# Moving two steps' sums into the chunk slots, spreading the first chunks' sums, and mixing less between the first chunks' stages

## The chip, the cores and the metric

The kernel runs on one core of a Trainium2 chip. The metric is the device time of one execution in microseconds. In the profiles TensorE is called PE (its weight loads PEld), VectorE DVE, ScalarE ACT, GpSimd POOL, and SyncE SP.

## The reference

A causal depthwise convolution over the sequence (7 taps, softmax weights for each of 8 heads) is followed by a mixer of phases: `theta = x @ w_theta`, then the token mix of `x cos(theta)` and `x sin(theta)` with two 4224 x 4224 matrices, then a channel mix.

```python
# x after the convolution: (8, 4224, 192)
theta = x @ w_theta
zr, zi = x * np.cos(theta), x * np.sin(theta)
y = np.einsum('ts,bsd->btd', w_tok_r, zr) + np.einsum('ts,bsd->btd', w_tok_i, zi)
u = x + y
out = u + np.maximum(u @ w_ch, 0.0)
```

The token mix is nearly all of the work. The kernel does it block by block with a seven-product scheme (Strassen-like), on 33 chunks of 128 input tokens and 58 steps.

## The kernel before

A *chunk* passes through a convolution (two halves), two transposes, two theta products with two sines each, two products and four sums (the "sums" of the title's second part). A *step* takes the chunks that are live (2 in step 0, then 4, 5, 7, 9, 11) through seven *runs* of mix pairs. A pair is two 128x384 matmuls that accumulate into a PSUM tile y. At the end of a run, y is copied (ACT) or added (DVE) into pv, the step's f32 sum tile in SBUF; this is a *give*. Two y tiles rotate in PSUM, and a run that opens a tile or goes on in one must wait until DVE or ACT has read what was there.

```python
def load_rows(self):                       # the step's sum tiles
    for tb in self.tbs:
        pv = wk.tile([P, N], F32, name="pv", tag="big", bufs=6)   # shares slots with xw
        ...
def give(self, y, i, h, copies):
    ...
    if self.first and copies:
        act(nc.scalar.activation(out=o, in_=yv, func=AT.Copy))          # L368
    else:
        dve(nc.vector.tensor_tensor(out=o, in0=yv, in1=o, op=ALU.add))  # L370
# (cut) the runs of a step: weights, z part, y tile, opens it?, (row block, half, may copy)
("11", Z11, "c1", True,  (0, 0, True)),  ("S1", T1, "c2", True,  (1, 1, True)),
("S2", T2,  "c1", False, (0, 1, True)),  ("S4", Z22, "c2", False, (0, 1, False)),
("S3", T3,  "c1", False, (1, 1, False)), ("12", Z21, "c3", True,  (0, 0, False)),
("22", T4,  "c1", False, (1, 0, True)),
```

The first eleven chunks must be made before the mix can run at full width. The start therefore interleaves: stage i convolves chunk i, finishes chunk i-1, and `between(n)` lets up to n mix pairs run, if their chunk is ready. The kernel ties the work of PE, DVE, ACT and POOL to this program order.

```python
for i in range(NW + 2):                    # NW = 11; ch = chunk i, old = chunk i-1
    def between(n):
        left = more(n)                     # n mix pairs, with the weight work and gives due
        if 0 < i < 3:
            idle(min(left, 2))             # matmuls on zeros, meant to keep PE's clock up
    if ch: ch.conv(0)
    between(3)
    if old: old.theta(0)
    between(2)
    if ch: ch.conv(1)
    ...
    between(3)
    if old: old.theta(1)
    ...                                    # load_chunk(i + 3)
    between(2)
    if ch: ch.transpose(0)
    if old: old.product(Z11)
    between(1)
    if ch: ch.transpose(1)
    between(1)
    if old:
        old.product(Z21)
        old.sums(0)                        # two DVE operations each
        old.sums(1)
    between(2)
```

## Time and profile before

| | before |
|---|---|
| time, median of the first 3 runs | 1474.13 us (1471.6 to 1476.81) |
| PE busy, whole span | 1435.7 of 1472.3 us |
| PE idle in 0-120 us (120 less the sum of PE busy in six stretches of 20 us) | 21.8 us |
| long PE waits for DVE at the start | 3.89, 1.20 and 3.29 us |

The head of the profile page, with the busy time of each engine:

```profile
span 1472.3 us, 24451 instructions
PE 1435.7 (98%) x10100; PEld 905.6 (62%) x10100; DVE 1001.1 (68%) x1050; ACT 361.1 (25%) x461; POOL 429.4 (29%) x659
```

PE is the engine to save time on. The table of stretches shows where it is not full. Columns: stretch, its length, then busy us (and instructions) of PE, PEld, DVE, ACT and POOL, the granted PE clock (1.00 is full), the DMA share and GB/s.

```profile
40.00:60.00 20.00, 14.95 (x124) 9.79 (x124) 12.77 (x20) 14.38 (x20) 8.87 (x16) 0.83 1.05 209
60.00:80.00 20.00, 19.35 (x181) 12.87 (x179) 19.00 (x29) 17.76 (x24) 9.39 (x17) 1.00 1.20 223
80.00:100.00 20.00, 17.67 (x164) 11.67 (x163) 16.66 (x22) 16.00 (x21) 6.38 (x12) 1.00 0.89 205
100.00:120.00 20.00, 16.71 (x103) 10.16 (x102) 19.46 (x23) 6.64 (x10) 4.86 (x9) 0.91 0.73 156
```

PE idles 5 us in 40-60 and 3.3 us in 100-120, and in both the clock is down as well: part of the time counted busy there was spent at half speed. The PE timeline names the waits (start, duration, engine, line, operation, output and inputs, shapes, count, and in brackets the idle time before with what ended it):

```profile
42.40 0.80 PE L405 MATMUL y<-z,wt 128*128 128x384 f16 x2 [3.89 <-DVE pv L370]
...
86.85 0.48 PE L405 MATMUL y<-z,wt 128*128 128x384 f16 x2 [1.20 <-DVE pv L370]
...
113.04 17.21 PE L405 MATMUL y<-z,wt 128*128 128x384 f16 x97 [3.29 <-DVE pv L370]
```

Two matmuls after the first wait take 0.80 us, two after the short one 0.48: the first pair runs at half clock. What DVE did during the first wait is in its timeline:

```profile
37.56 0.95 DVE L238 TENSOR_TENSOR z<-z 128x1536 f16<-128x1536 f16 x1
38.55 2.34 DVE L244 TENSOR_TENSOR z<-z 128x768 f16<-128x768 f16 x4
40.80 0.70 DVE L308 STREAM_TRANSPOSE wt<-st 128x512 f16<-128x512 f16 x1
41.43 0.92 DVE L370 TENSOR_TENSOR pv<-y,pv 128x768 f32<-128x768 f32 x1
```

One chunk's product, its four sums and a weight transpose stand in the queue ahead of the addition that PE waits for (L370). PE goes on at 42.40, when that addition is done.

### The profile page before, as it was taken

How to read it: one execution, taken by the hardware profiler on the slowest of the kernel's cores; microseconds unless marked ns; L12 is line 12 of the kernel's file. 1: busy time of each engine (PE TensorE's matmuls, PEld its weight loads, DVE VectorE, ACT ScalarE, POOL GpSimd, SP SyncE). 2: the span in 40 equal slices, each digit the busy share in tenths (PEclk: the TensorE clock that was granted, in tenths of full speed). 3: DMA queues.
4: the chain of work that ended last, by engine and by line, in shares of the span. 5: the costliest groups of instructions: out<-in, count | busy, mean ns of one | idle time of the engine just before them, and what ended most of it. 6: DMA issues, size and time to landing. Idle time of an engine off the chain costs nothing.

```text
span 1472.3 us, 24451 instructions
## 1 busy us (share of the span) xinstructions
PE 1435.7 (98%) x10100; PEld 905.6 (62%) x10100; DVE 1001.1 (68%) x1050; ACT 361.1 (25%) x461; POOL 429.4 (29%) x659
## 2 busy tenths in 40 slices
PE   7899999999999999999999999999999999999997
PEld 5565666666666666566666656666666666666664
DVE  6784545454548687766666657778787778778585
ACT  5771111111134254000000005245122222222234
POOL 7422211121233232211112323332224243544220
PEclk9999999999999999999999999999999999999999
DMA  9986657465699999987779989999778777999873
GB/s 165 201 187 145 130 98 152 95 145 102 120 246 218 214 243 241 202 215 152 215 154 224 226 184 231 191 229 263 144 176 200 190 177 180 211 253 223 198 200 109
DMA packets 234975, 274.16 MB, mean 186 GB/s; under 512 B 69104, under 2 KB 202608, under 8 KB 234864
## 3 DMA queue, kind: packets, MB, share of 16 engines
q0 software_dynamic: 163616, 95.30, 49.1%
q1 hardware_dynamic: 71248, 177.30, 33.9%
q8 instruction: 79, 1.29, 0.3%
q14 instruction: 32, 0.26, 0.1%
HBM read 245.49 MB, written 111.28 MB: 242 GB/s over the span
## 4 chain that ended last, share of the span: by engine, by line
PE 87%; DMA 5%; DVE 4%; ACT 1%; issue 1%; SPq 0%; POOL 0%; DVEq 0%; ACTq 0%; POOLq 0%
PE y L405 78%; PE v L138 5%; PE tp L153 2%; PE pc L196 2%; DVE pv L370 1%; DVE wt L308 1%; DMA part<-pv 1%; DMA xw<-xw 1%; DMA st<-in_moe_w_tok_i_dram 1%; DVE z L244 1%; DMA xw<-in_x_dram 1%; ACT z L233 1%; DVE z L238 1%; DMA pv<-part 1%; DVE pv L434 0%
## 5 line engine op out<-in xcount | busy, mean ns | idle before, releaser
L405 PE MATMUL y<-z,wt 128*128 128x384 f16 x7656 | 1297.6, 326 | 12.4 <-DVE pv L370 11.6
L405 PEld LDWEIGHTS <-wt 128*128 128x128 f16 x7656 | 738.4, 98 | 481.6 <-issue 17.5
L370 DVE TENSOR_TENSOR pv<-y,pv 128x768 f32<-128x768 f32 x324 | 308.6, 953 | 376.2 <-PE y L405 362.9
L308 DVE STREAM_TRANSPOSE wt<-st 128x1408 f16<-128x1408 f16 (+7 forms) x224 | 326.5, 1463 | 4.8 <-DMA st<-in_moe_w_tok_i_dram 4.6
L295 POOL DMA_DIRECT2D st<-in_moe_w_tok_i_dram x232 | 132.5, 579 | 502.9 <-DVE wt L308 487.6
L295 POOL DMA_DIRECT2D st<-in_moe_w_tok_r_dram x232 | 132.5, 579 | 467.1 <-DVE wt L308 447.8
L320 DVE TENSOR_TENSOR wt<-wt 128x1408 f16<-128x1408 f16 (+7 forms) x216 | 204.0, 945 | 10.9 <-PE y L405 8.2
L148 ACT ACTIVATE uT<-tp 128x768 f16<-128x768 f16 x127 | 102.2, 814 | 294.9 <-PE tp L153 293.3
L148 ACT ACTIVATE z<-pc 128x768 f16<-128x768 f32 x65 | 52.9, 813 | 387.0 <-PE pc L196 387.0
L368 ACT ACTIVATE pv<-y 128x768 f32<-128x768 f32 x66 | 53.6, 815 | 280.1 <-PE y L405 279.8
L138 PEld LDWEIGHTS <-uT 128*128 128x128 f16 x1056 | 91.8, 98 | 24.0 <-issue 8.3
L434 DVE SCALAR_TENSOR_TENSOR pv<-v,pv 128x768 f32<-128x768 f32 x66 | 62.6, 950 | 44.3 <-PE v L138 42.1
L183 POOL DMA_DIRECT2D xw<-in_x_dram x132 | 76.1, 584 | 28.3 <-DMA st<-in_moe_w_tok_r_dram 9.8
L424 ACT ACTIVATE ub<-pv 128x768 f16<-128x768 f32 x66 | 54.8, 837 | 90.2 <-DVE pv L370 89.2
L244 DVE TENSOR_TENSOR z<-z 128x768 f16<-128x768 f16 x132 | 73.5, 557 | 4.2
L233 ACT ACTIVATE z<-v,half_pi 128x768 f16<-128x768 f32 x66 | 59.5, 902 | 45.9 <-PE v L138 45.9
L238 DVE TENSOR_TENSOR z<-z 128x1536 f16<-128x1536 f16 x66 | 60.6, 949 | 13.4 <-ACT z L233 13.4
L352 POOL TENSOR_TENSOR pv<-pv,xr 128x1536 f32<-128x1536 f32 x20 | 62.5, 3124 | 7.6 <-issue 6.9
L138 PE MATMUL v<-wch,uT 128*128 128x192 f16 x528 | 54.2, 246 | 3.9 <-DVE pv L434 2.2
L138 PE MATMUL v<-wth,uT 128*128 128x192 f16 x528 | 55.3, 248 | 1.4 <-ACT z L233 1.3
L233 ACT ACTIVATE z<-v 128x768 f16<-128x768 f32 x66 | 53.1, 805 | 0.0
L153 PE MATMUL tp<-ident,z 128*128 128x128 f16 x396 | 33.4, 222 | 6.3 <-ACT z L233 6.2
(43 smaller groups left out, 203.0 us busy)
## 6 DMA issues: line engine op xcount, KB each, us to landing
part<-pv SPq DMA_DIRECT2D x79, 768.0 KB, 4.1
pv<-part SPq DMA_DIRECT2D x79, 768.0 KB, 5.4
out_dram<-pv SPq DMA_DIRECT2D x66, 384.0 KB, 4.4
st<-in_moe_w_tok_r_dram POOLq DMA_DIRECT2D x136, 176.0 KB, 6.0
st<-in_moe_w_tok_i_dram POOLq DMA_DIRECT2D x136, 176.0 KB, 4.8
xs<-z SPq DMA_DIRECT2D x132, 96.0 KB, 4.3
xw<-in_x_dram POOLq DMA_DIRECT2D x121, 96.0 KB, 5.8
part<-xs POOLq DMA_DIRECT2D x26, 384.0 KB, 6.9
```

The costliest lines, as they stand in the source:

```text
L138: pe(nc.tensor.matmul(v[:, k, b * D : (b + 1) * D], lhsT=tT[:, 3 * k + b + i, :], rhs=w[:, 2 * b + i, :], start=(i == 0), stop=(i == 1),))
L148: act(nc.scalar.activation(out=out, in_=in_, func=AT.Copy))
L153: pe(nc.tensor.transpose(tp[:, 0, k * P : (k + 1) * P], u[:, k * P : (k + 1) * P], ident))
L183: nc.gpsimd.dma_start(out=self.xw[lo : lo + n, h, :, :], in_=x[:, t0 : t0 + n, :].rearrange("b s d -> s b d"),)
L233: act(nc.scalar.activation(**args))
L238: dve(nc.vector.tensor_tensor(out=o, in0=xv, in1=o, op=ALU.mult))
L244: dve(nc.vector.tensor_tensor(out=z[:, o, :], in0=z[:, a, :], in1=z[:, b, :], op=ALU.subtract))
L295: pool(nc.gpsimd.dma_start(out=st[a * Q : (a + 1) * Q, 0:nb, :, 0:n] .rearrange("i r bt s -> i (r bt) s"), in_=w[self.tbs[0] * P : (self.t ...
L308: dve(nc.vector.transpose(self.w[name][:, 0 : self.n, :, :], self.st[int(name[1])][:, int(name[0]) - 1, :, 0 : self.n * Q] .rearrange("p b ...
L320: dve(nc.vector.tensor_tensor(out=self.w[name][:, 0 : self.n, :, :], in0=self.w[a][:, 0 : self.n, :, :], in1=self.w[b][:, 0 : self.n, :, : ...
L370: dve(nc.vector.tensor_tensor(out=o, in0=yv, in1=o, op=ALU.add))
L405: pe(nc.tensor.matmul(y[cn][:, q, 0:BH], lhsT=self.w[wn][:, c, :, :].rearrange("p bt i -> p (bt i)"), rhs=chunks[k].z[:, zn, q * BH : (q + ...
```

## The change

It has three parts. (A) The sum tiles pv of steps 0 and 1 go into slots of later chunks, which are still free then, so that they no longer hold back the loads of chunks. (B) Ten mix pairs instead of fourteen run in each of the first stages. (C) The two halves of a chunk's sums are queued with mix pairs, and so with gives, between them. Nothing is computed differently.

```diff
         def load_rows(self):
             for tb in self.tbs:
-                pv = wk.tile([P, N], F32, name="pv", tag="big", bufs=6)
+                if self.t < 2:
+                    pv = zpool.tile([P, N], F32, name="pv", tag="z")
+                else:
+                    pv = wk.tile([P, N], F32, name="pv", tag="big", bufs=6)
...
         if ch:
             ch.conv(0)
-        between(3)
+        between(2)
         if old:
             old.theta(0)
-        between(2)
+        between(1)
         if ch:
             ch.conv(1)
...
-        between(3)
+        between(2)
         if old:
             old.theta(1)
...
-        between(2)
+        between(1)
         if ch:
             ch.transpose(0)
...
         if ch:
             ch.transpose(1)
+        if old:
+            old.product(Z21)
         between(1)
         if old:
-            old.product(Z21)
             old.sums(0)
+        between(1)
+        if old:
             old.sums(1)
-        between(2)
+        between(1)
```

## The prediction

> **What bounds the kernel now.** The tensor engine. The profile page has PE busy 1435.7 us of a 1472.3 us span (98%). The table of stretches puts nearly all PE idle time at the start: 5.6 us in 0-20, 4.9 in 20-40, 5.1 in 40-60, 0.7 in 60-80, 2.3 in 80-100, 3.3 in 100-120, then none up to 400. The granted clock is 0.83 in 40-60 and 0.91 in 100-120, elsewhere 1.0. So a change to the first eleven chunks can win some 20 us of 1474, under 2%.
>
> Three gaps matter (PE timeline, "y<-z,wt waits for DVE pv"): 3.9 us ending at 42.4, 1.2 ending at 86.85, 3.3 ending at 113.0. In each, the DVE timeline has one chunk's four sums (2.34 us) just ahead of the addition into pv (0.95) that PE needs before it may write that PSUM tile again. After the first and third the clock is about 0.5 for 4.7 and 3 us: some 2.3 and 1.5 us more lost. The Trainium skill, "TensorE: Matmul & The Clock Gate", "What's actually happening", says that the clock falls to half after an idle window of about 3.4 us; the trace agrees (3.9 and 3.3 us did it, 1.2 did not).
>
> **What the change does.** No arithmetic is added or removed, except two idle matmuls fewer in each of two stages (-0.5 us).
> - Mix pairs per stage fall from 14 to 10. A pair is 0.325 us of PE, so a stage loses 1.3 us of mixing. Some 30 pairs (9.8 us) move behind the last stage, where PE is dense: no gain in itself. Stages of 8.2 us (conv to conv, 58 to 83 us) become shorter, but for a chunk ACT needs about 5.9 us plus 0.7 per copy of y, about 6.8; DVE 6.5; PE 6.6. I expect 7.2 to 7.5, with ACT's latency showing as PE waits: 0.4 us more idle in 7 stages, +3 us.
> - Sums are placed differently against the step ends. The third gap goes, because step 3 now ends after all chunk sums (-3.3, -1.5 of clock). The second goes (-1.2): its addition is queued a stage ahead of its reader. The first stays in part: DVE still has about 8 us of work in chunk 3's stage ahead of the addition that PE waits for; I estimate 3 us instead of 3.9, and half a chance that the clock stays up (-2 in all).
> - The pv tiles of steps 0 and 1 in chunk slots free four uses of the "big" buffers: chunk loads start earlier. PE waited only 0.2 us for such a load: no gain in itself; it keeps loads ahead of faster stages. Sixteen tiles now go through eleven slots: chunks 9 and 10 need step 1's pv written out (landing 3.2 to 7.6 us), with about 8 us for it: at most a short wait of ACT.
>
> Sum: -4.8 -1.2 -2 -0.5 +3 = about -5.5 us.
>
> **Predicted: 1469 us, 8 in 10 between 1463 and 1475. Faster by over 2%: 1%; within 2%: 98%; slower by over 2%: 1%.**
>
> **What the profile would show.** Stage spacing 7.2-7.5 us; the wait near 110 us gone and the clock 1.0 there; a PE wait for DVE pv of 2-3.5 us left near 37-41 us; more short PE waits for ACT z and uT between 45 and 100 us; dense mixing beginning about 8 us earlier; stretches from 130 us on unchanged.
>
> **What would make it wrong.** The first gap growing, with a longer cold stretch; ACT waiting for step 1's pv to leave a slot; so many small waits that the clock falls more often; chunk loads held behind weight loads on POOL. Each would cost 2 to 6 us. Or the first gap closing wholly: 3 us more.

## More of the kernel before

The view of waits adds up the start, 0 to 117 us (waiting engine, its line, what ended the wait: us in total, times, longest):

```profile
PE y L405 <- DVE pv L370: 8.4, 3, 3.9
PE tp L153 <- ACT z L233: 6.2, 9, 1.4
...
PE v L138 <- ACT z L233: 0.8, 3, 0.5
```

Long waits for DVE come first, short ones for ACT second. One event is the same in all kernels of this study: the ACT copy that ends step 3, the last step of the start. Its start is called **E3** below. In the kernel before it is 116.80 us. The second fixed point is the first group of transposes after a PE gap of 1.69 us near the end. From there to the end is the **tail**.

```profile
116.80 0.81 ACT L368 ACTIVATE pv<-y 128x768 f32<-128x768 f32 x1 [10.29 <-PE y L405]
```

The stretches 0 to E3, E3 to the tail, and the tail (same columns as above):

```profile
0.00:116.80 116.80, 94.98 (x806) 62.36 (x807) 90.10 (x142) 77.09 (x103) 56.78 (x109) 0.96 1.05 186
116.80:1459.55 1342.75, 1335.61 (x9239) 838.94 (x9237) 906.35 (x904) 280.16 (x355) 372.59 (x550) 1.00 0.82 186
1459.55:1472.30 12.75, 5.13 (x58) 4.29 (x58) 4.69 (x5) 3.84 (x5) 0.00 (x0) 0.94 0.55 185
```

## The result

The change measured 1471.05 us, the median of 4 runs (1469.78 to 1471.56), against 1473.31 (1471.6 to 1476.81, 4 runs) for the kernel before. The ratio is 0.998, with a 95% interval of 0.996 to 1.0. Ratios here are the mean time of one kernel's fast runs over that of the other's fast runs of the same rounds, so they are not quite the ratios of the quoted medians. With more rounds later the ratio was 0.9977 (0.9964 to 0.999).

The same views of the profile after. The head of the page:

```profile
span 1469.8 us, 24434 instructions
PE 1434.6 (98%) x10095; PEld 905.6 (62%) x10095; DVE 1001.0 (68%) x1050; ACT 360.7 (25%) x461; POOL 430.3 (29%) x659
```

Five idle matmuls fewer (10100 to 10095), the rest as before. The stretches of the start:

```profile
40.00:60.00 20.00, 16.07 (x158) 10.72 (x158) 16.01 (x25) 17.69 (x25) 11.42 (x20) 1.00 1.18 231
60.00:80.00 20.00, 17.32 (x169) 11.04 (x167) 17.05 (x25) 16.75 (x23) 6.83 (x12) 1.00 1.11 236
80.00:100.00 20.00, 18.07 (x153) 11.92 (x152) 17.79 (x26) 16.18 (x23) 4.48 (x8) 1.00 0.71 167
100.00:120.00 20.00, 18.98 (x118) 11.34 (x116) 15.66 (x17) 3.79 (x5) 6.76 (x12) 1.00 0.80 160
```

The clock is now 1.00 in every stretch. PE idles less in 40-60 and 100-120, and more in 60-80 (2.7 us where it was 0.7). The long waits on the PE timeline:

```profile
40.33 0.49 PE L408 MATMUL y<-z,wt 128*128 128x384 f16 x2 [1.79 <-DVE pv L373]
...
65.16 0.48 PE L408 MATMUL y<-z,wt 128*128 128x384 f16 x2 [0.91 <-DVE pv L373]
...
107.54 22.75 PE L408 MATMUL y<-z,wt 128*128 128x384 f16 x139 [1.02 <-DVE pv L373]
```

Three waits again, all shorter. DVE ahead of the first of them now does the sums in two halves with two weight sums between them, and then an addition into pv (that of run S4, where it was that of S3 before):

```profile
36.34 1.15 DVE L244 TENSOR_TENSOR z<-z 128x768 f16<-128x768 f16 x2
37.40 0.95 DVE L320 TENSOR_TENSOR wt<-wt 128x512 f16<-128x512 f16 x2
38.27 1.14 DVE L244 TENSOR_TENSOR z<-z 128x768 f16<-128x768 f16 x2
39.33 0.95 DVE L373 TENSOR_TENSOR pv<-y,pv 128x768 f32<-128x768 f32 x1
```

The waits, 0 to 117 us:

```profile
PE tp L153 <- ACT z L233: 8.3, 10, 1.1
PE y L408 <- DVE pv L373: 3.7, 3, 1.8
PE v L138 <- ACT z L233: 2.5, 8, 0.6
...
PE y L408 <- ACT pv L371: 0.8, 1, 0.8
```

Waits for DVE fell by 4.7 us (8.4 to 3.7). Waits for ACT's sines grew by 3.8 (6.2 + 0.8 to 8.3 + 2.5). E3 is 112.29 us:

```profile
112.29 0.81 ACT L371 ACTIVATE pv<-y 128x768 f32<-128x768 f32 x1 [9.47 <-PE y L408]
```

The three stretches:

```profile
0.00:112.29 112.29, 90.62 (x801) 59.63 (x802) 88.65 (x141) 76.69 (x102) 56.91 (x109) 1.00 1.03 184
112.29:1454.83 1342.54, 1335.62 (x9238) 838.94 (x9237) 907.53 (x905) 280.14 (x355) 373.40 (x550) 1.00 0.82 187
1454.83:1469.80 14.97, 8.36 (x58) 6.98 (x58) 4.79 (x5) 3.84 (x5) 0.00 (x0) 0.64 0.46 158
```

This comparison raises two questions. First, up to E3 the change is 4.51 us ahead, but PE is idle as long as before: 116.80 - 94.98 = 21.82 us against 112.29 - 90.62 = 21.67. What shrank is *busy* time, by 4.36 us, with the same work and five idle matmuls less (5 x 0.163 = 0.8 us). Second, the long middle is equal within 0.2 us, and the tail then gives back 2.2 us: its 58 matmuls and transposes are busy 8.36 us instead of 5.13, at a granted clock of 0.64.

### The profile page after: what moved, and what is told of

Its sections match the earlier page's. It is cut to its first block, busy times and chain, and to the rows that moved or that the text cites. A ratio compares the mean times of both kernels' runs of the same rounds, so it can differ in the third digit from the quotient of the medians.

```text
span 1469.8 us, 24434 instructions
## 1 busy us (share of the span) xinstructions
PE 1434.6 (98%) x10095; PEld 905.6 (62%) x10095; DVE 1001.0 (68%) x1050; ACT 360.7 (25%) x461; POOL 430.3 (29%) x659
## 4 chain that ended last, share of the span: by engine, by line
PE 91%; DVE 3%; ACT 3%; DMA 1%; issue 1%; POOL 0%; DVEq 0%; ACTq 0%; POOLq 0%
PE y L408 81%; PE v L138 6%; PE tp L153 3%; ACT z L233 2%; PE pc L196 2%; DMA st<-in_moe_w_tok_i_dram 1%; DVE pv L373 1%; DVE z L244 1%; DVE z L238 0%; DVE wt L308 0%; DVE pv L437 0%; ACT uT L148 0%; DVE wt L320 0%; ACT pv L371 0%; ACT z L148 0%
```

## The experiments

The theories, as they were formed on the two traces:

- **O**: order on DVE and the number of pairs (part B) make the gain. **L**: earlier chunk loads (part A) do. **S**: the spread sums (part C) do.
- **P**: the tail's length is chance: the clock falls over the sparse work there in some executions and not in others. **D**: it belongs to the kernel.
- **C**: what was gained up to E3 is time at half clock, not waiting. **W**: it is the shorter waits themselves.
- **A**: in the shortened stages ACT's amount of work sets the pace and gave back the idle time. **V**, **L2**, **V2**: its latency, or other waits.

Eleven kernels ran in three batches, each with its own runs of the kernel before: medians 1472.4 (11 runs), 1474.49 (11) and 1473.76 us (9). All gave correct results. The table gathers them; the paragraphs below read it.

| kernel | E3 | tail | median us | ratio to before (95%) |
|---|---|---|---|---|
| before, first trace | 116.80 | 12.75 | see text | 1 |
| after, first trace | 112.29 | 14.97 | 1471.05 | 0.998 (0.996 to 1.0) |
| after_again | 113.16 | 12.56 | 1470.64 | 0.9977 (0.9964 to 0.999) |
| a_only | 116.46 | 13.53 | 1475.19 | 1.0009 (0.9997 to 1.0021) |
| b_only | 113.20 | 14.92 | 1471.38 | 0.9983 (0.9971 to 0.9995) |
| c_only | 115.88 | 15.13 | 1474.23 | 1.0002 (0.9989 to 1.0015) |
| no_a (B and C) | 112.25 | 12.49 | 1469.4 | 0.9971 (0.9959 to 0.9984) |
| before_filled | 113.02 | 13.87 | 1469.97 | 0.9974 (0.9962 to 0.9986) |
| warm_tail | 112.06 | 12.58 | 1469.33 | 0.9966 (0.9953 to 0.9979) |
| act_relief | 114.84 | 13.53 | 1472.7 | 0.999 (0.9973 to 1.0007) |
| shift_pairs | 108.55 | 13.58 | 1468.02 | 0.9958 (0.9944 to 0.9971) |
| late_w | 111.52 | 12.51 | 1469.61 | 0.997 (0.9957 to 0.9982) |
| best | 109.36 | 12.52 | 1464.96 | 0.9942 (0.993 to 0.9955) |

Two cautions on E3, which is from one trace of each kernel. The first convolution starts at 10.3 us in ten of these traces, but at 9.2 in warm_tail and shift_pairs and at 9.5 in act_relief, so those three are about 1 us early there: the 32 small matmuls just ahead of it took 1.57 us in the three and about 2.64 in the ten. And the first mix pair starts at 24.69 us in the kernel before, at 23.83 in the first trace of the change, and at 23.85 in a_only, which has the order and the counts of the kernel before. In the kernel before the 8 conv matmuls at 14.7 us took 0.92 us, in a_only 0.59; half clock is the likely reason, though the clock column reads 1.00 there. So 0.86 of the change's 4.51 us were there before its first mix pair, most likely by chance, and 3.65 came after it.

### The change again (after_again)

No edit.

> The changed kernel again, to see what repeats. Two numbers are read from each trace: E3, the start of the copy that ends step 3 (116.80 us before, 112.29 in the first trace of the change), and the tail, from the transposes after the 1.7 us PE gap near the end to the end of the span (12.75 us before with the clock up, 14.97 after with the clock at half for about 10 us). Theory P (phase): the start is the same in every execution, E3 112.3 within 0.5, and the tail is 12.7 or about 15 by chance[...], so that totals of either kernel spread over 2 us or more and the gain of 4.5 us is seen as anything from 2 to 6.5. Rival D (deterministic): the tail of the changed kernel is always about 15 and that of the kernel before always 12.75; totals then 2.5 us apart in every round.

The kernel is the same and the trace is not. E3 is 113.16, not 112.29, and the tail 12.56, not 14.97. In this execution the clock stayed up better in the tail and fell near 42 us instead, after the same 1.79 us wait for DVE. E3 moved 0.87 us, more than theory P had allowed for the start, because the start is subject to the same chance. A stretch of 2 us, which begins 1.7 us after that wait ended, shows it (the clock there is 0.50):

```profile
42.00:44.00 2.00, 2.00 (x12) 1.60 (x11) 0.87 (x1) 0.21 (x2) 2.00 (x5) 0.50 0.89 119
```

The times of the runs say the same. Of the 31 runs of the kernel before in the three batches, the one with a mean granted clock of 0.998 took 1470.62 us, the eleven with 0.996 took 1472.48 on average, and the six with 0.993 took 1475.71. Over all 31 runs, time and clock correlate with -0.77; one run breaks the rule, with 1471.13 us at 0.994. The five runs of the change here: 1468.88 at clock 1.000, 1469.68 at 0.998, and 1470.64 to 1471.42 at 0.997. Rival D is dead, and the clock goes with most of the spread between runs of one kernel.

It also goes with most of the difference between the kernels. In this batch the mean clock was 0.9952 before (11 runs) and 0.9978 after (5 runs). The clock time lost is about (1 - 0.9952) x 1472 = 7.1 us against (1 - 0.9978) x 1468 = 3.2 us: an estimate of 3.8 us, where the mean times differ by 3.1 us (1473.45 to 1470.33). That is a correlation; before_filled below is the test.

### One part at a time (a_only, b_only, c_only, no_a)

Each takes hunks of the diff above: a_only the hunk in `load_rows`, b_only the four changed counts, c_only the last hunk with the other counts as before; no_a is everything but the hunk in `load_rows`.

> Only the sums tiles of steps 0 and 1 move to the chunks' slots. Theory O (order on DVE and the number of pairs make the gain): nothing moves at the start, E3 116.3 to 117.0, the 3.9 us wait for DVE near 42 us and the half clock after it stay, total as before within 1.5 us. Rival L (earlier chunk loads make it, because the chain of waits of before holds landings of part and xw copies): E3 falls by 2 us or more.

E3 116.46, with the 3.89 us wait at 41.55 in place and a 3.65 us wait at 111.78; the ratio is 1.0009. The clock fell here too (0.91 in 40-60 us, 0.83 in 100-120), though the pair just behind the 3.89 us wait still took 0.48 us. Part A alone does nothing that can be told from zero. Its median is above that of before; the interval includes 1, and its five runs all had a clock of 0.993 to 0.995.

> Only the numbers of mix pairs fall, 14 to 10 a stage. Theory O: this alone does nearly all, because it moves the reader of DVE's addition behind it by a stage's worth of other work: first wait about 2 us in place of 3.9 with the clock staying at 1.0, no wait with half clock at step 3; E3 112 to 113.5. Rival L: without the freed buffers the shorter stages wait for chunk loads: PE or the evacuations wait for xw near 60 to 90 us, E3 not under 115. Rival S (the spreading of the sums does it): E3 115 or more.

E3 113.20, with the first wait 1.92 us, the last 1.30, and no PE wait for a chunk's load listed between 50 and 100 us. Part B alone reproduces after_again (113.16). As there, the clock fell near 42 us in the profiled run, contrary to the expectation that it would stay up.

> Only the sums are spread, with the pairs per stage kept at 14. Theory O: DVE has the same work ahead of the addition that PE waits for at the end of step 0 and of step 3, so the waits near 42 and 112 us stay (3 to 4 us each, half clock after the first): E3 115.5 to 117. Rival S: the waits shrink to under 2 us with the clock up: E3 112 to 114.

E3 115.88. The first wait is split in two (0.90 and 2.77 us) and the last is still 3.29; the clock is 0.83 in 40-60 us and 0.91 in 100-120, as before. The ratio is 1.0002. Part C alone does nothing, as theory O said.

> The change without the moved sums tiles: fewer pairs and spread sums only. Theory O: the moved tiles do nothing for the time, because PE never waits for a chunk's load with or without them: E3 112.3 to 113.2, total 1470 to 1471.5, no wait for xw over 0.3 us. Rival L (the faster stages need the earlier loads): waits for xw of 1 us or more appear between 45 and 92 us, E3 over 114.

E3 112.25 and ratio 0.9971: the change without part A is as good as the change. Chunk loads never held PE for more than 0.3 us. So of the three parts, the fewer pairs (B) carry the whole effect, and rivals L and S fall. Why fewer pairs help can be read from the order in the two first traces, but was not tested by itself. At the first wait, both kernels wait for an addition that stands just behind a chunk's sums. Counted from the conv that opens this stage (37.11 us before, 35.71 after), PE comes to the waiting pair after 2.83 us instead of 1.40, because a theta product and a wait of 0.81 us for ACT now lie ahead of it; and the addition is done after 4.57 us instead of 5.24. Together these are the 2.10 us by which the wait shrank. At the third wait, the last chunk's sums began at 109.78 us before, right ahead of the addition at 112.03; in the change they began at 99.19, with five weight operations between them and the addition at 106.54.

### The clock without the shorter waits (before_filled)

The kernel *before* with its order kept. Idle matmuls that nothing reads are put in front of the two pairs that wait long, writing to a rotating PSUM tile of the chunk work. Splitting `between(3)` also lets one more idle matmul run in each of stages 1 and 2, so that 44 matmuls are added in all (10144 instead of 10100).

```diff
+    def fill(n):
+        f = banks("fill")
+        for _ in range(n):
+            pe(nc.tensor.matmul(f[:, 0, 0:BH], lhsT=ident,
+                rhs=wth[:, 0:2, :].rearrange("p a d -> p (a d)"), start=True, stop=True))
...
             ch.conv(0)
-        between(3)
+        between(2)
+        if i == 4:
+            fill(10)
+            fill(12)
+        between(1)
...
-        between(2)
+        between(1)
+        if i == 12:
+            fill(10)
+            fill(10)
+        between(1)
         if ch:
             ch.transpose(0)
```

> The kernel before, with its order kept, and idle matmuls that nothing reads put into the two long PE gaps (22 just ahead of the 3.9 us wait near 42 us, 20 ahead of the 3.3 us wait near 113 us; 0.163 us each). No wait is shortened by this. Theory C (the gain of the change up to the end of step 3 is less time at half clock, not less waiting: in the two first traces PE is idle 21.8 us before that point with the kernel before and 21.7 with the change): the clock stays at 1.0 in 40-60 and 100-120 us, E3 falls from 116.8 to about 113 us, the total to about that of the change, 1470 to 1471 us. Rival W (the gain is the shorter waits themselves): E3 stays at 116 or more and the total within 1 us of the kernel before.

The PE timeline shows the first gap filled. The real pair behind it starts 0.52 us earlier than in the kernel before, but still when DVE's addition releases it. That lead is not from the filler: this trace had it at its first mix pair (24.69 us before, 24.18 here; these are the first of the lines below).

```profile
24.69 0.50 PE L405 MATMUL y<-z,wt 128*128 128x384 f16 x2
```

```profile
24.18 0.50 PE L405 MATMUL y<-z,wt 128*128 128x384 f16 x2
...
37.82 3.74 PE L544 MATMUL fill<-wth,ident 128*128 128x384 f16 x22
41.88 0.48 PE L405 MATMUL y<-z,wt 128*128 128x384 f16 x2 [0.32 <-DVE pv L370]
```

It then takes 0.48 us where it took 0.80. The stretch around it, and E3:

```profile
40.00:60.00 20.00, 16.84 (x157) 11.12 (x156) 14.47 (x23) 16.45 (x23) 9.14 (x16) 1.00 1.09 210
```

```profile
113.02 0.81 ACT L368 ACTIVATE pv<-y 128x768 f32<-128x768 f32 x1 [8.99 <-PE y L405]
```

The clock is 1.00 in this stretch, and so it is in 100-120 us (0.91 before). E3 falls from 116.80 to 113.02, and the ratio is 0.9974: as good as the whole change, with the real pairs waiting as long as before and 44 useless matmuls more. Theory C holds and W falls. Counted from the first mix pair to E3, so that the chance of the first 24 us is left out, the change gains 3.65 us (88.46 instead of 92.11) and the filled kernel 3.27 (88.84): some nine tenths of the gain are had by the clock alone. The second trace of the change, whose clock fell near 42 us, gains 2.63 by this count.

### The tail (warm_tail)

The changed kernel with 20 idle matmuls in the PE gaps of the last stretch.

```diff
-    for at, f in sorted(outputs, key=lambda e: e[0]):
-        if at >= sum(s.time for s in steps):
-            f()
+    rest = [f for at, f in sorted(outputs, key=lambda e: e[0])
+            if at >= sum(s.time for s in steps)]
+    warm = ypool.tile([P, 2, PC], F32, name="y", tag="y")
+    fill = {0: 8, 4: 5, 6: 4, 9: 3}
+    for n, f in enumerate(rest):
+        f()
+        for _ in range(fill.get(n, 0)):
+            pe(nc.tensor.matmul(warm[:, 0, 0 : 2 * D], lhsT=ident,
+                rhs=wch[:, 0:2, :].rearrange("p a d -> p (a d)"), start=True, stop=True))
```

> The changed kernel with 20 idle matmuls that nothing reads in the PE gaps of the last 14 us. Theory P (the tail's 12.6 or 15 us is the clock falling by chance over those gaps): the clock stays at 1.0 to the end in all runs, tail 12.6, total 1468.5 to 1469.8 with a smaller spread than the change (1468.9 to 1471.6). Rival D (the tail is long for another reason, such as the output stores): tail and total as with the change, 1470.6 median.

The tail's stretch:

```profile
1454.22:1466.80 12.58, 7.08 (x70) 5.37 (x70) 4.70 (x5) 3.84 (x5) 0.00 (x0) 1.00 0.55 188
```

The clock is 1.00, the tail 12.58 us, and the five runs lie within 1468.45 to 1469.66. Eleven of the thirteen traces have no idle matmuls in the tail. Their tails run from 12.49 to 15.13 us with a mean of 13.6, so the filler is worth about 1 us on average (an estimate from these eleven). Both kernels are open to this chance; that the first trace of the change lost 2.2 us here is not an effect of the change.

### Where the idle time went (act_relief, shift_pairs)

The waits for ACT's sines grew as those for DVE shrank. The prediction had named ACT's latency for these waits, but had worked out the length of a stage from ACT's amount of work. act_relief tests the latter: one of a chunk's two ACT copies of transposed x goes to DVE.

```diff
-                self.x[:, g * GC : (g + 1) * GC], 0 < self.k < 3 or (self.k, g) == (0, 1)
+                self.x[:, g * GC : (g + 1) * GC], 0 < self.k < 3 or (self.k < NW and g == 1)
```

> The changed kernel with one of each chunk's two copies of transposed x moved from ACT (0.76 us a piece) to DVE (0.56). Theory A (in the shortened stages ACT's round of about 6.8 us of work plus 1.1 us of waiting for PE sets the spacing of 7.9 us, and is what gave back the idle time won at the long waits): spacing of the convs between 46 and 85 us falls to 7.2 to 7.5, PE waits for ACT's z there fall from 4.5 us to under 2, E3 falls by 1 to 2 us. Rival V (DVE or PE order sets it): spacing stays 7.7 to 8.1, or PE waits for DVE grow by as much as those for ACT fall, E3 unchanged within 0.5.

ACT has less to do (71.5 us busy up to E3 instead of 76.7) and nothing gets faster. The convs still come 7.92 us apart from 71.62 to 87.46, and the wait for the sines hardly changed, while that for DVE grew:

```profile
PE tp L153 <- ACT z L233: 7.6, 9, 1.1
PE y L408 <- DVE pv L373: 5.6, 3, 2.9
```

The longer wait for DVE (2.88 us near 40 us) also brought the clock down again, to 0.84 in 40-60 us; it was also down in 0-20 us (0.83), so E3 is no clean measure here. The unchanged spacing is: theory A falls. The wait is latency: PE reaches the second transposes before the two sines of the second theta are done, and the change took a pair away from between them. In the kernel before that wait is 0.38 us in a regular stage, in the change 0.70; a pair is 0.325.

shift_pairs keeps ten pairs a stage but puts two of them there:

```diff
             load_chunk(i + 3)
-        between(1)
+        between(3)
...
             old.product(Z21)
         between(1)
         if old:
             old.sums(0)
-        between(1)
-        if old:
             old.sums(1)
-        between(1)
```

> The changed kernel with the same ten pairs a stage, two of them moved from the end of the stage to between the second theta and the transposes. Theory L2 (the small waits that the change added are latency: PE reaches the second transposes before ACT's two sines of the second theta, 1.6 us, are done, and the change took one 0.325 us pair from between them, so the wait rose from 0.38 to 0.70 a stage; moving a copy from ACT to DVE left that at 0.70): the wait of the transposes for ACT's z in the stages from 53 us on falls from about 0.7 to under 0.15 each, the convs come 7.2 to 7.6 us apart, and E3 falls by 1.5 to 3 us to 109.5 to 111. Rival V2 (what is taken there comes back at the stage's other waits, since ACT's round is the same): spacing 7.8 to 8.0 us and E3 within 0.7 of 112.2.

The waits up to 117 us:

```profile
PE y L408 <- DVE pv L373: 3.3, 2, 1.9
PE tp L153 <- ACT z L233: 3.1, 5, 0.9
PE v L138 <- ACT z L233: 2.7, 9, 0.6
PE pc L196 <- ACT uT L148: 2.6, 4, 0.9
...
PE y L408 <- ACT pv L371: 2.4, 3, 1.1
```

The transposes' wait fell from 8.3 to 3.1 us, and 3.7 us came back at other places (pc for uT 0.5 to 2.6, y for ACT's copies 0.8 to 2.4). Two stages of the five regular ones wait not at all, three 0.44 us, more than the 0.15 expected. The convs come 7.54 us apart on average (43.55 to 81.26 over five stages) against 7.84 in the change (46.03 to 85.24). E3 is 108.55, or 2.6 us earlier than in the change once the start of the first conv is taken off (108.55 - 9.22 against 112.29 - 10.34). Its ratio to the kernel before, 0.9958, lies below the change's 0.9977, with overlapping intervals. L2 is right in kind; V2 is right that some two thirds of such a saving in waits come back. The listed waits account for about 1.5 of the 2.6 us. Some 0.6 us lie before the first mix pair (22.15 us, where the change has 23.83), in part because the moved counts leave two idle matmuls out (10093); the rest was not traced.

### DVE's queue ahead of the addition (late_w), and all together (best)

In step 0, four weight operations of step 1 are put behind the additions (and the load that needs their buffer with them):

```diff
-            found += steps[t + 1].w_tasks()
+            late = {3.05: 6.5, 3.3: 6.6, 4.2: 6.7, 5.1: 6.8} if t == 0 else {}
+            found += [(late.get(at, at), f) for at, f in steps[t + 1].w_tasks()]
...
-                found.append((1.3 + 3 * (m - 1), lambda m=m: nxt.load_w(m)))
+                at = 6.9 if t == 0 and m == 2 else 1.3 + 3 * (m - 1)
+                found.append((at, lambda m=m: nxt.load_w(m)))
```

> The changed kernel with four of step 1's weight operations (two sums 0.95 us together, a transpose 0.70, a sum 0.42) put behind step 0's additions on DVE. Theory O (DVE's queue ahead of the addition sets the wait near 40 us): the 1.8 us wait falls to 0.5 to 1.1 and step 0 ends 1.2 us earlier; with the gap short the clock stays at 1.0 in 40-60 us in most runs; E3 111.0 to 111.5; total about 1 us under the change. Rival: the wait stays, or the weights then come late and PE waits for them near 45 to 50 us by as much.

The wait near 40 us falls from 1.79 to 1.05, E3 to 111.52, and the clock stays at 1.00 throughout the start. The median is 1469.61. Two of the five runs had a clock of 1.000 (1467.95 and 1468.86), three 0.996 or 0.997: the clock still falls somewhere in most runs.

best is the change with late_w, shift_pairs and warm_tail together.

> All three additions to the change together: the moved pairs, the late weight operations of step 1 and the idle matmuls in the tail. If L2, O and P hold, they add up: E3 108.5 to 110, tail 12.6 with the clock up, total 1465.5 to 1467.5, against 1470.6 for the change. If the shorter start is given back later, the total stays at that of the change with idle matmuls in the tail, 1469.3.

It measured 1464.96 us (1464.61 to 1466.14), ratio 0.9942 (0.993 to 0.9955): clearly faster than the kernel before, and the interval does not touch that of the change (0.9964 to 0.999). Its five runs had a clock of 0.999 or 1.000. E3 is 109.36 and the tail 12.52, both as expected, and the total is just under the expected range. best ran against the kernel before, not in one batch with the change.

## Why the prediction was right

The measured time lies inside the range, and nearly all probability was on "within 2%", which held. The range also holds the kernel before (1474.13 and 1473.31 us), so to land in it says little. The direction was right too. The sum of about -5.5 us was too large for what came out (-2.3 by the first medians, -3.1 by the means of the later batch), and its terms fared unevenly.

- **The ceiling.** Right. Everything outside the first 120 us and the tail is equal within 0.2 us, so only the start's 20 us were to be had.
- **The third gap goes, -3.3 and -1.5 of clock.** Mostly right: 1.02 us of wait remain (so -2.3), and the clock is 1.00 there in both traces of the change.
- **The second gap goes, -1.2.** Gone at its place, but a wait of the same kind, 0.91 us, came up at the end of step 1. The net is -0.3.
- **The first gap: 3 us left, and half a chance for the clock, -2 in all.** The wait was 1.79 us, shorter than the 2 to 3.5 announced. The half chance was a guess that turned out apt: of the five traces with a wait of 1.79 to 1.92 us there, the clock held in two (the first of the change, no_a) and fell in three (after_again, b_only, warm_tail).
- **+3 us from ACT's latency in shorter stages.** Right in kind and nearly in size: the waits for ACT's sines grew by 3.8 us, and shift_pairs, which cut the transposes' wait from 8.3 to 3.1 us by putting two pairs ahead of it, speaks for latency. The stage length of 7.2 to 7.5 us was missed: it measured 7.84. It had been worked out from the work of the engines, ACT's (6.8 us) the longest; act_relief took work off ACT and the spacing stayed.
- **Four idle matmuls fewer, -0.5.** It was five, 0.8 us at most.
- **No gain from the moved sum tiles.** Right: a_only has 1.0009, no_a 0.9971.
- **What was missing** is the weight of the clock. The prediction listed clock terms of -1.5 and part of -2 beside waiting terms of the same size. The experiments show the waiting terms summing to about nothing (PE idle up to E3 21.8 and 21.7 us), and the clock making nearly all of the gain (before_filled: 3.27 of 3.65 us from the first mix pair to E3). It also took the rule that a gap must reach about 3.4 us to bring the clock down, from the page that it cites and three waits of one trace; after gaps of 1.7 to 1.9 us it fell in some executions. The tail, open to the same chance, was left out, and cost the first trace of the change 2.2 us.

Not settled: what exactly in the recent activity of PE brings the clock down. From 20 us to E3, over all thirteen traces, it fell during or soon after each of the seven waits for DVE of 2.77 to 3.89 us, after three of the five of 1.79 to 1.92 us near 40 us, not after one of 1.90 us near 103 us (shift_pairs), and after none of 1.53 us or less.

## What to carry to other kernels

When a PE-bound kernel has gaps, price each as the wait plus the half-clock time behind it, and look at both before moving work about: here nearly the same idle time in smaller pieces (15.3 and 14.8 us from the first mix pair to E3) took 3.1 us off PE's busy time, and a few idle matmuls in the old gaps were worth as much as the reordering. When matmuls are taken out of a pipelined stage, ask which latency they covered: taking one pair from between a product and the transposes that wait for its sines exposed about that pair's length in each regular stage (0.38 us of wait became 0.70). And when a kernel's run times spread, sort them by granted clock before comparing medians.

## What the Trainium skill lacked or had wrong

- "TensorE: Matmul & The Clock Gate", sections "What's actually happening" and "Why this matters for your kernels": they put the fall of the clock at an idle window of about 3.4 us and advise to avoid gaps over about 3 us. Here the clock went to half after PE waits of 1.79 us (after_again, with PE busy 0.47 of the 2 us before 40 us), 1.92 us (b_only) and 1.69 us (the tail of the change), each amid sparse work. In other executions of the same kernel the same waits left it at 1.00. This goes against the two sections only: the page's section "A second HAM failure mode: psum-queue depth-cycling" does report a clock that goes up and down over frequent short idles.
- The same page says that the clock's window runs freely and that the number of slow matmuls varies from run to run. The runs here agree that it varies; that the window runs freely, none of them shows. They add the size for a kernel that is 98% PE-busy: one kernel spreads from 1470.62 us (mean clock 0.998) to 1476.8 (0.993).
- "Perfetto Trace Analysis", section "Optimization Strategy", advises to find the gaps and make their dependencies start sooner or complete faster. No page of it that was read says that idle matmuls in a gap on PE can be worth as much: 42 of them, with the real pairs waiting as long as before, gave a ratio of 0.9974 here.
